# Local attention and a phase-mixing layer on one core: the last head pair of the first batch in two-head pieces, the first steps reordered, the weight loads reordered

## The chip, the core and the metric

The kernel runs on one core of a Trainium2 chip. The metric is the device time of one execution in microseconds. Four runs of the kernel before gave a median of 172.93 us, between 172.67 and 173.31 us. One further execution was recorded by the hardware profiler; it took 172.37 us, of which the span from the first to the last instruction is 170.2 us, so 2.2 us lie around the span.

The core has five engines that run side by side, each in the order of its own queue: the tensor engine (PE, with weight loads shown as PEld), the vector engine (DVE), the scalar engine (ACT), GpSimd (POOL) and SyncE (SP). They meet through semaphores. Transfers are issued by SP, ACT or POOL and run on sixteen shared DMA engines.

## What is computed

Four batches of 768 tokens. First an attention with 8 heads of 64 features, in which a token sees the 96 tokens before it and the first 8 tokens, with a bias that falls with distance. Then a layer that turns the result by angles, mixes it over tokens with two 768 x 768 matrices and over channels with a 512 x 512 matrix:

```python
scores = scale * q @ k.T + bias          # masked: local window of 96, or one of the first 8 keys
a = softmax(scores)
x = (a @ v)                              # B, S, H*D = 4, 768, 512
theta = x @ w_theta
zr, zi = x * cos(theta), x * sin(theta)
y = w_tok_r @ zr + w_tok_i @ zi          # over tokens
u = x + y
out = u + relu(u @ w_ch)
```

## The kernel before

Tokens are tiled in six tiles of 128 (`NT = 6`), heads in four pairs (`NP = 4`), the 512 channels in four blocks of 128 (`NC = 4`); pair `p` of heads fills channel block `p` of x.

The first batch is written out by hand, instruction by instruction, in the order of lines 535 to 618, and every engine keeps that order. Everything after it (the mixing of batch b woven with the attention of batch b+1) is ordered by a scheduler, apart from the last tiles.

For a pair `p` of the first batch the steps are these. `turn0` (L209) transposes q and k of two heads on PE, 12 transposes each, and `out0` (L213) copies the results out of PSUM as qT (on DVE) and kT (on ACT). `kglob` (L221) makes kG, copies of the key tiles whose first 8 columns are those of the global keys, with two DVE copies. Scores come in three chunks `c` of two token tiles: `score_bias` (L278) writes the bias into a PSUM tile with two matmuls, `score_mms` (L287) adds the products, `score_exp` (L309) takes the exponential on ACT. The chunks 0 and 1 take 8 score matmuls, the chunk 2 takes 6. `vglob` (L335) makes vG, the value tiles with the global rows, for four heads at a time with two DVE copies. `values` (L346) multiplies by the values for one head; a 65th column of ones gives the sum of the softmax, and DVE takes the reciprocal (`rec`, L371) and multiplies (`x_sb`, L373). `xtrans` (L375) transposes x of a pair on PE and copies it out of PSUM as xT. In batches 1 to 3 `xtrans` is a DMA transpose from the SP queue instead, except for the last pair of batch 1, which goes over PE and an ACT copy.

`theta` (L390) multiplies xT by w_theta, for two token tiles at a time: `theta(b, c, 2)` takes the channel blocks 0 to 2 and `theta(b, c, 3)` the last one, because the last pair of heads is the last to be ready. `sines` (L410) takes cosine and sine on ACT (`cs`) and multiplies by x on DVE (`zri`). `trans_w` (L165) transposes one row block of the two token matrices from `w_nat` on PE and copies it out as `w_tokT`. `mix` (L424) is the multiplication over tokens, `utrans` (L439) and `chan` (L451) the last step. The sine functions and the exponential need different tables on ACT; `sine_table` (L306) loads the one for sines with a dummy activation.

The weights are loaded by `load_w` (L153), from the POOL queue: w_theta first, then pairs of row blocks of the two token matrices, the q and k of batch 1, and w_ch. A load waits at its issue until the load eight places before it has landed. PSUM has four small tiles (`ps`, one bank each) and two large ones (`pb`, two banks each), handed out in turn; a step that takes one waits until its last reader is through.

Of the kernel before, what the change touches and what calls it, by code (L numbers as in the profile page):

```python
# [9 lines left out]
FP = mybir.dt.float32  # L10
# [6 lines left out]
def kernel(  # L17
# [13 lines left out]
    nc = tc.nc  # L31
    B, H, S, D = q.shape
    T = 128
    NT = S // T
    DM = H * D
    NC = DM // T
    NP = H // 2
# [18 lines left out]
    def ps_small(shape, dtype):  # L56
        return small.tile(shape, dtype, name="ps", tag="ps")
# [40 lines left out]
    for i_, eng in ((1, nc.sync), (0, nc.scalar)):  # L98
        eng.dma_start(out=qk32[:, i_].rearrange("p h t d -> p h (t d)"),
                      in_=(q, k)[i_][0, 0:2].rearrange("h (p t) d -> p h (t d)", p=T))  # L100
# [47 lines left out]
    w_theta_bf = const.tile([T, NC, DM], BF)  # L148
# [2 lines left out]
    w_tokT = [const.tile([T, NT, S], BF, name=f"w_tokT_{wi}") for wi in range(2)]  # L151

    def load_w():  # L153
        nc.gpsimd.dma_start(out=w_theta_bf, in_=moe_w_theta.rearrange("(c p) n -> p c n", p=T))
        for tt in range(0, NT, 2):
            for wi, src in enumerate((moe_w_tok_r, moe_w_tok_i)):
                w2 = moe.tile([T, 2, S], BF, name="w_nat", bufs=6)
                nc.gpsimd.dma_start(
                    out=w2, in_=src[tt * T:(tt + 2) * T, :].rearrange("(a p) s -> p a s", p=T))
                w_nat[wi, tt], w_nat[wi, tt + 1] = w2[:, 0], w2[:, 1]  # L160
            if tt == NT - 4:
                load_all_qk(1)
        nc.gpsimd.dma_start(out=w_ch_bf, in_=moe_w_ch.rearrange("(c p) n -> p c n", p=T))
# [29 lines left out]
    def behind(eng):  # L193

        return tc.issue_after(anchor[eng]) if eng in anchor else nullcontext()
# [17 lines left out]
    def out0(p, i_, copy, half=None):  # L213
        to = qkT.setdefault((0, p), [None, None, None])
        if to[i_] is None:
            to[i_] = att.tile([T, S], BF, name=("qT", "kT")[i_], tag=("qT", "kT")[i_], bufs=6)
        ns = slice(0, T) if half is None else slice(half * T // 2, (half + 1) * T // 2)
        copy(out=to[i_].rearrange("p (n t) -> p n t", t=NT)[:, ns],  # L218
             in_=tiles0[p, i_].rearrange("p t n -> p n t")[:, ns])

    def kglob(b, p, t0=0, t1=NT - 2, copy=nc.vector.tensor_copy):  # L221
        kT = qkT[(b, p)][1]
        if t0 == 0:
            qkT[(b, p)][2] = att.tile([T, NT - 2, T], BF, name="kG", bufs=6)
        kG = qkT[(b, p)][2][:, t0:t1]
        with behind("zri" if p else "dve") if b == B - 1 else nullcontext():
            copy(  # L227
                out=kG, in_=kT[:, (t0 + 1) * T:(t1 + 1) * T].rearrange("p (t n) -> p t n", t=t1 - t0))
            copy(out=kG[:, :, 0:NG], in_=kT[:, None, 0:NG].to_broadcast([T, t1 - t0, NG]))  # L229
# [48 lines left out]
    def score_bias(p, c):  # L278
        pb = pbs[0, p, c] = ps_big()
        n = min(4, 2 * NT - 1 - 4 * c)  # L280
        s0 = 2 if c else 0
        for hh in range(2):
            nc.tensor.matmul(pb[:, hh, 0:n * T], lhsT=diag[:, 2 * p + hh],
                             rhs=dist[:, s0:s0 + n].rearrange("p s n -> p (s n)"),
                             start=True, stop=False)
# [20 lines left out]
    def sine_table():  # L306
        nc.scalar.activation(junk, halfpi, AF.Sin)
# [25 lines left out]
    vGs, pos = {}, {}  # L333

    def vglob(b, h0, n):  # L335

        vn = loads[b][1]
        if h0 == 0:
            vGs[b] = att.tile([T, H, NT - 2, D + 1], BF, name="vG", bufs=1)
        hs = slice(h0, h0 + n)  # L340
        vG = vGs[b]
        with behind("dve"):
            nc.vector.tensor_copy(out=vG[:, hs], in_=vn[:, hs, 1:NT - 1, :])
        nc.vector.tensor_copy(out=vG[0:NG, hs], in_=vn[0:NG, hs, 0:1, :].to_broadcast([NG, n, NT - 2, D + 1]))

    def values(b, p, hh, i0=0, i1=NT):  # L346
        vn = loads[b][1]
        e_t, vG = ebuf[(b, p)], vGs[b]
        h = 2 * p + hh
        if b == 0:  # L350
            po = ps_small([T, 1, 512], FP)
        else:
            if hh == 0:
                pos[(b, p)] = ps_big()
            po = pos[(b, p)][:, hh:hh + 1, :]
        for it in range(i0, i1):
            mms = [(e_t[:, hh, it, 0, :], vn[:, h, it, :])]
            if it:
                mms.append((e_t[:, hh, it - 1, 1, :], vG[:, h, it - 2, :] if it > 1 else vn[:, h, 0, :]))
            o = po[:, 0, (it - i0) * (D + 1):(it - i0 + 1) * (D + 1)]  # L360
            for i_, (l_, r_) in enumerate(mms):
                nc.tensor.matmul(o, lhsT=l_, rhs=r_, start=(i_ == 0), stop=(i_ == len(mms) - 1))  # L362
        if b and hh == 0:
            return
        if b:
            po = pos[(b, p)]
        h0, n = (hh, 1) if b == 0 else (0, 2)
        nt = i1 - i0
        po4 = po[:, :, 0:nt * (D + 1)].rearrange("p a (t d) -> p a t d", d=D + 1)
        rec = att.tile([T, n, NT, 1], FP, name="rec", tag=f"rec{n}")[:, :, 0:nt]  # L370
        nc.vector.reciprocal(rec, po4[:, :, :, D:D + 1])  # L371
        xv = x_sb[b][:, p, i0:i1, h0 * D:(h0 + n) * D].rearrange("p t (a d) -> p a t d", a=n)
        nc.vector.tensor_mul(xv, po4[:, :, :, 0:D], rec.to_broadcast([T, n, nt, D]))  # L373

    def xtrans(b, p, copy=nc.vector.tensor_copy, i0=0, i1=NT):  # L375
        if b > 1 or (b and p < 3):
            anchor["sp"] = nc.sync.dma_start_transpose(
                out=xT_sb[b][:, p, :].rearrange("p (t s) -> p t s", t=NT),
                in_=x_sb[b][:, p].rearrange("p t d -> p (t d)")).ins
            return  # L380
        ps = ps_small([T, S], BF)
        own = slice(i0 * T, i1 * T)
        for st in range(i0, i1):
            nc.tensor.transpose(ps[:, st * T:(st + 1) * T], x_sb[b][:, p, st, :], ident)
        copy(out=xT_sb[b][:, p, own], in_=ps[:, own])
# [4 lines left out]
    def theta(b, c, j):  # L390
        last0 = [(j_, NC - 1) for j_ in range(2)]
        part = {0: [(0, dc) for dc in range(NC - 1)],
                1: [(1, dc) for dc in range(NC - 1)] + last0,
                2: [(j_, dc) for j_ in range(2) for dc in range(NC - 1)],
                3: last0}[j]
        if c == 0 and j in (0, 2):
            zri[b] = moe.tile([T, 2, NT, DM], BF, name="zri", tag="zri", bufs=1)
        xT, xb = xT_sb[b], x_sb[b]
        last = c == NT // 2 - 1
        if j in (0, 2):  # L400
            pss["th", c] = [ps_small([T, DM], FP) for _ in range(2)] if last else ps_big()
        pb = pss["th", c]
        st = lambda j_: slice((2 * c + j_) * T, (2 * c + j_ + 1) * T)
        for j_, dc in part:
            nc.tensor.matmul(pb[j_] if last else pb[:, j_, :], lhsT=xT[:, dc, st(j_)],  # L405
                             rhs=w_theta_bf[:, dc, :], start=(dc == 0), stop=(dc == NC - 1))
        if j == 1:
            sines(b, c)
# [59 lines left out]
    def load_all_qk(b):  # L468
        alloc_qk(b)
        load_qk(b, 0, 8)  # L470
# [63 lines left out]
    dve, act = nc.vector.tensor_copy, nc.scalar.copy  # L534
# [26 lines left out]
    for p in range(NP - 1):  # L561
        score_exp(0, p, 1)
        out0(p + 1, 1, act)
        out0(p + 1, 0, dve)
        kglob(0, p + 1)
        score_bias(p, 2)
        score_mms(0, p, 2)
        if p:
            values(0, p - 1, 0)
            values(0, p - 1, 1)  # L570
        score_exp(0, p, 2)
        if p < 2:
            vglob(0, 4 * p, 4)
        score_bias(p + 1, 0)
        score_mms(0, p + 1, 0)
        if p + 2 < NP:
            turn0(p + 2, 1)
            turn0(p + 2, 0)
        score_exp(0, p + 1, 0)
        score_bias(p + 1, 1)  # L580
        score_mms(0, p + 1, 1)
        if p == 1:
            xtrans(0, 0)
    p = NP - 1
    score_exp(0, p, 1)
    values(0, p - 1, 0)
    xtrans(0, p - 2)
    values(0, p - 1, 1)
    score_bias(p, 2)
    score_mms(0, p, 2)  # L590
    score_exp(0, p, 2)
    trans_w(0, act, False, act)
    sine_table()
    xtrans(0, p - 1, dve)
    values(0, p, 0, 0, 4)
    values(0, p, 1, 0, 4)
    theta(0, 0, 2)
    xtrans(0, p, dve, 0, 4)
    values(0, p, 0, 4, 6)
    values(0, p, 1, 4, 6)  # L600
    theta(0, 0, 3)
    xtrans(0, p, dve, 4, 6)
    sines(0, 0)
    theta(0, 1, 2)
    theta(0, 1, 3)
    theta(0, 2, 2)
    theta(0, 2, 3)
    trans_w(1, dve, True)
# [97 lines left out]
```

## Time and profile before

| what | value |
|---|---|
| four runs, median (lowest to highest) | 172.93 us (172.67 to 173.31) |
| profiled execution: time, span | 172.37 us, 170.2 us |
| PE busy, share of the span | 157.6 us, 93% |
| DVE busy | 125.9 us, 74% |
| ACT busy | 100.8 us, 59% |
| POOL busy | 37.8 us, 22% |
| DMA of the POOL queue (q0) | 12.45 MB in 45680 packets |
| DMA of the SP queue (q1) | 12.52 MB in 28176 packets |
| granted PE clock | full speed in all slices |

Times in the profile count from the start of the span. The page gives averages; which engine sets the end changes from stage to stage, so a change at one place is read from the waits of that stage: what starts when, and what it waited for. PE's matmuls overlap: one of 128x512 is shown with some 380 ns, but the next may start 216 ns after it, so gaps on PE are read from the starts.

### The profile page before, as it was taken

How to read it: one execution, taken by the hardware profiler on the slowest of the kernel's cores; microseconds unless marked ns; L12 is line 12 of the kernel's file. 1: busy time of each engine (PE TensorE's matmuls, PEld its weight loads, DVE VectorE, ACT ScalarE, POOL GpSimd, SP SyncE). 2: the span in 40 equal slices, each digit the busy share in tenths (PEclk: the TensorE clock that was granted, in tenths of full speed). 3: DMA queues.
4: the chain of work that ended last, by engine and by line, in shares of the span. 5: the costliest groups of instructions: out<-in, count | busy, mean ns of one | idle time of the engine just before them, and what ended most of it. 6: DMA issues, size and time to landing. Idle time of an engine off the chain costs nothing.

```text
span 170.2 us, 3718 instructions
## 1 busy us (share of the span) xinstructions
PE 157.6 (93%) x1516; PEld 84.2 (49%) x1540; DVE 125.9 (74%) x267; ACT 100.8 (59%) x129; POOL 37.8 (22%) x45
## 2 busy tenths in 40 slices
PE   7478998999999999999999999999999999999991
PEld 2255574565646456445555463444554644444440
DVE  6646976598999999967998788588776856614432
ACT  4697787997587576399944550899348309400010
POOL 8966347003192110497000000000000000000000
PEclk9999999999999999999999999999999999999999
DMA  4999999999999999999997678779145472222435
GB/s 152 201 173 178 208 209 203 206 208 179 151 205 183 190 141 179 127 156 196 145 119 86 140 171 129 166 139 262 35 77 139 112 168 78 111 60 43 148 92 185
DMA packets 74288, 25.73 MB, mean 151 GB/s; under 512 B 62368, under 2 KB 71328, under 8 KB 74272
## 3 DMA queue, kind: packets, MB, share of 16 engines
q0 software_dynamic: 45680, 12.45, 78.9%
q1 hardware_dynamic: 28176, 12.52, 33.2%
q10 hardware_dynamic: 416, 0.52, 1.0%
q8 instruction: 12, 0.20, 0.5%
q14 instruction: 4, 0.03, 0.1%
HBM read 25.69 MB, written 6.29 MB: 188 GB/s over the span
## 4 chain that ended last, share of the span: by engine, by line
PE 65%; DVE 19%; DMA 7%; ACT 6%; issue 1%; DVEq 0%
PE ps L430 30%; PE ps L458 9%; PE pb L405 7%; PE pb L303 5%; DMA xT<-x_sb 4%; PE ps L405 4%; PE pb L362 3%; DVE qT L257 3%; DMA qk<-in_k_dram 2%; DVE e L322 2%; ACT e L313 2%; DVE x_sb L373 2%; PE ps L207 2%; DVE e L325 1%; DVE kG L227 1%
## 5 line engine op out<-in xcount | busy, mean ns | idle before, releaser
L430 PE MATMUL ps<-zri,w_tokT 128*128 128x512 bf16 x273 | 67.7, 380 | 1.1 <-issue 0.3
L313 ACT ACTIVATE e<-pb 128x1024 bf16<-128x1024 f32 (+1 forms) x48 | 43.7, 954 | 18.4 <-PE pb L303 17.9
L430 PEld LDWEIGHTS <-w_tokT 128*128 128x128 bf16 x288 | 25.9, 98 | 28.1 <-DVE w_tokT L175 0.6
L435 DVE TENSOR_TENSOR u<-x_sb,ps 128x512 bf16<-128x512 bf16 x24 | 16.3, 680 | 11.0 <-PE ps L430 10.8
L458 PE MATMUL ps<-w_ch_bf,uT 128*128 128x512 bf16 (+1 forms) x97 | 24.2, 371 | 0.2
L419 DVE TENSOR_TENSOR zri<-x_sb,cs 128x1024 bf16<-128x1024 bf16 (+1 forms) x30 | 16.6, 581 | 6.5 <-ACT cs L415 6.4
L463 DVE SCALAR_TENSOR_TENSOR o_sb<-ps,u 128x512 f32<-128x512 f32 (+1 forms) x25 | 16.4, 663 | 4.1 <-PE ps L458 3.6
L415 ACT ACTIVATE cs<-pb,halfpi 128x1024 bf16<-128x1024 f32 x8 | 8.9, 1114 | 16.4 <-PE pb L405 16.4
L303 PE MATMUL pb<-qT,kT 64*128 64x128 bf16 x224 | 15.4, 220 | 2.4 <-DVE qT L218 1.3
L322 DVE TENSOR_TENSOR e<-e,etab 128x1024 bf16<-128x1024 bf16 (+1 forms) x24 | 14.8, 618 | 3.1 <-ACT e L313 3.0
L303 PEld LDWEIGHTS <-kT 64*128 64x128 bf16 x224 | 8.9, 94 | 14.9 <-issue 12.1
L405 PE MATMUL pb<-w_theta_bf,xT 128*128 128x512 bf16 x61 | 15.0, 380 | 1.0 <-DMA xT<-x_sb 0.6
L362 PEld LDWEIGHTS <-e 128*128 128x128 bf16 x352 | 12.8, 97 | 4.3 <-issue 1.8
L449 ACT COPY uT<-ps 128x512 bf16<-128x512 bf16 x7 | 4.2, 594 | 18.2 <-PE ps L448 18.2
L405 PEld LDWEIGHTS <-xT 128*128 128x128 bf16 x96 | 8.9, 98 | 12.1 <-DMA xT<-x_sb 2.1
L458 PEld LDWEIGHTS <-uT 128*128 128x128 bf16 x100 | 9.0, 98 | 9.7 <-ACT uT L449 0.8
L88 POOL DMA_DIRECT2D vn<-in_v_dram x5 | 9.6, 1928 | 14.1 <-DVE qkn L238 12.4
L303 PE MATMUL pb<-qT,kG 64*128 64x128 bf16 x128 | 11.5, 217 | 0.5 <-DVE kG L229 0.5
L373 DVE TENSOR_TENSOR x_sb<-pb,rec 128x768 bf16<-128x768 f32 x12 | 11.4, 953 | 0.3
L362 PE MATMUL pb<-vn,e 128*128 128x65 bf16 x168 | 9.7, 193 | 0.6 <-DVE x_sb L373 0.3
L325 DVE TENSOR_TENSOR e<-e,etab 128x1024 bf16<-128x1024 bf16 x12 | 8.2, 687 | 2.4 <-ACT e L313 2.4
L259 ACT COPY kT<-ps 128x768 bf16<-128x768 bf16 x8 | 6.4, 797 | 4.6 <-PE ps L253 4.4
(76 smaller groups left out, 203.1 us busy)
## 6 DMA issues: line engine op xcount, KB each, us to landing
out_dram<-o_sb SPq DMA_DIRECT2D x23, 256.0 KB, 2.4
vn<-in_v_dram POOLq DMA_DIRECT2D x3, 768.0 KB, 21.0
qk<-in_q_dram POOLq DMA_DIRECT2D x2, 768.0 KB, 20.6
qk<-in_k_dram POOLq DMA_DIRECT2D x2, 768.0 KB, 23.6
w_nat<-in_moe_w_tok_r_dram POOLq DMA_DIRECT2D x3, 384.0 KB, 14.8
w_nat<-in_moe_w_tok_i_dram POOLq DMA_DIRECT2D x3, 384.0 KB, 14.0
vn<-in_v_dram POOLq DMA_DIRECT2D x2, 384.0 KB, 9.7
qk<-in_q_dram POOLq DMA_DIRECT2D x8, 96.0 KB, 9.1
```

The source lines that it names most:

```text
L303: nc.tensor.matmul(pb[:, hh, o:o + T], lhsT=lhsT, rhs=qT[R, (own, nxt)[part]], start=bool(b), stop=bool(b) or (jt == NT - 1 or (j == 1 and ...
L313: ins = nc.scalar.activation(e_c, pb[:, :, 0:n], AF.Exp, scale=scale).ins
L322: nc.vector.tensor_mul(e_c, e_c, tab[:, :, s0:s0 + n // T].rearrange("p a s n -> p a (s n)"))
L325: nc.vector.tensor_mul(e4, e4, tab[:, :, 2:4].rearrange("p a s n -> p a (s n)")[:, :, None, :].to_broadcast([T, 2, 2, 2 * T]))
L362: nc.tensor.matmul(o, lhsT=l_, rhs=r_, start=(i_ == 0), stop=(i_ == len(mms) - 1))
L373: nc.vector.tensor_mul(xv, po4[:, :, :, 0:D], rec.to_broadcast([T, n, nt, D]))
L405: nc.tensor.matmul(pb[j_] if last else pb[:, j_, :], lhsT=xT[:, dc, st(j_)], rhs=w_theta_bf[:, dc, :], start=(dc == 0), stop=(dc == NC - 1))
L419: anchor["zri"] = nc.vector.tensor_mul(zri[b][:, i_, 2 * c + j_:2 * c + j_ + n, :].rearrange("p j (g d) -> p j g d", g=NP), xb[:, :, 2 * c ...
L430: anchor["pe"] = nc.tensor.matmul(ps, lhsT=w_tokT[wi][:, st, tt * T:(tt + 1) * T], rhs=zri[b][:, wi, st, :], start=(st == 0 and wi == 0), ...
L435: anchor["dve"] = nc.vector.tensor_add(u_sb[b, tt].rearrange("p (g d) -> p g d", g=NP), x_sb[b][:, :, tt, :], ps.rearrange("p (g d) -> p g ...
L458: nc.tensor.matmul(ps_c, lhsT=uT[:, dc, :], rhs=w_ch_bf[:, dc, i_ * n:(i_ + 1) * n], start=(dc == 0), stop=(dc == NC - 1))
L463: nc.vector.scalar_tensor_tensor(o_sb[:, cols], in0=ps_c, scalar=0.0, in1=u[:, cols], op0=ALU.max, op1=ALU.add)
```

## The change

The pieces of the diff:

- `load_w` issues the first row blocks of the two token matrices ahead of w_theta.
- `values` can take both heads of a pair at once (`hh` is None) for a range of tiles in one PSUM tile, with one reciprocal and one multiplication. The last pair of batch 0 uses it in three pieces of two token tiles, instead of one piece of four tiles and one of two for each head.
- `theta` has two new parts, 4 (channel blocks 0 and 1) and 5 (block 2). For the first two token tiles they run apart, around the first two pieces of the last pair. Part 2 goes over the blocks with the two token tiles inside, not the other way round.
- In the loop over pairs, `turn0` of the next but one pair stands after the scores of chunk 1 of the next pair; for pair 3 the qT copy stands before the xT copy of pair 0, and the second `vglob` after kG of pair 3 (it stood before both).
- After the loop, the transposes of pair 1 stand behind the scores of the last chunk, and their copy is on ACT instead of DVE; the sine table is loaded ahead of the copies of `trans_w(0)`.
- `xtrans` takes the last pair of batch 2 over PE and an ACT copy as well; it was a DMA transpose.

```diff
     def load_w():
-        nc.gpsimd.dma_start(out=w_theta_bf, in_=moe_w_theta.rearrange("(c p) n -> p c n", p=T))
         for tt in range(0, NT, 2):
...
                 w_nat[wi, tt], w_nat[wi, tt + 1] = w2[:, 0], w2[:, 1]
+            if tt == 0:
+                nc.gpsimd.dma_start(out=w_theta_bf, in_=moe_w_theta.rearrange("(c p) n -> p c n", p=T))
...
     def values(b, p, hh, i0=0, i1=NT):
...
-        h = 2 * p + hh
+        nt = i1 - i0
         if b == 0:
-            po = ps_small([T, 1, 512], FP)
+            h0, n = (0, 2) if hh is None else (hh, 1)
+            po4 = ps_small([T, 512], FP)[:, 0:n * nt * (D + 1)].rearrange("p (a t d) -> p a t d", a=n, d=D + 1)
...
+        for head in range(2) if hh is None else (hh,):
+            h = 2 * p + head
+            for it in range(i0, i1):
...
     def xtrans(b, p, copy=nc.vector.tensor_copy, i0=0, i1=NT):
-        if b > 1 or (b and p < 3):
+        if b > 2 or (b and p < NP - 1):
...
-                2: [(j_, dc) for j_ in range(2) for dc in range(NC - 1)],
-                3: last0}[j]
+                2: [(j_, dc) for dc in range(NC - 1) for j_ in range(2)],
+                3: last0,
+                4: [(j_, dc) for dc in range(NC - 2) for j_ in range(2)],
+                5: [(j_, NC - 2) for j_ in range(2)]}[j]
...
     for p in range(NP - 1):
         score_exp(0, p, 1)
         out0(p + 1, 1, act)
-        out0(p + 1, 0, dve)
+        if p < 2:
+            out0(p + 1, 0, dve)
         kglob(0, p + 1)
+        if p == 2:
+            vglob(0, 4, 4)
         score_bias(p, 2)
         score_mms(0, p, 2)
         if p:
             values(0, p - 1, 0)
             values(0, p - 1, 1)
         score_exp(0, p, 2)
-        if p < 2:
-            vglob(0, 4 * p, 4)
+        if p == 0:
+            vglob(0, 0, 4)
         score_bias(p + 1, 0)
         score_mms(0, p + 1, 0)
+        score_exp(0, p + 1, 0)
+        score_bias(p + 1, 1)
+        score_mms(0, p + 1, 1)
         if p + 2 < NP:
             turn0(p + 2, 1)
             turn0(p + 2, 0)
-        score_exp(0, p + 1, 0)
-        score_bias(p + 1, 1)
-        score_mms(0, p + 1, 1)
         if p == 1:
+            out0(3, 0, dve)
             xtrans(0, 0)
     p = NP - 1
     score_exp(0, p, 1)
     values(0, p - 1, 0)
-    xtrans(0, p - 2)
-    values(0, p - 1, 1)
     score_bias(p, 2)
     score_mms(0, p, 2)
     score_exp(0, p, 2)
+    xtrans(0, p - 2, act)
+    values(0, p - 1, 1)
+    sine_table()
     trans_w(0, act, False, act)
-    sine_table()
-    xtrans(0, p - 1, dve)
-    values(0, p, 0, 0, 4)
-    values(0, p, 1, 0, 4)
-    theta(0, 0, 2)
-    xtrans(0, p, dve, 0, 4)
-    values(0, p, 0, 4, 6)
-    values(0, p, 1, 4, 6)
+    xtrans(0, p - 1)
+    values(0, p, None, 0, 2)
+    theta(0, 0, 4)
+    xtrans(0, p, dve, 0, 2)
+    values(0, p, None, 2, 4)
+    theta(0, 0, 5)
     theta(0, 0, 3)
-    xtrans(0, p, dve, 4, 6)
-    sines(0, 0)
+    xtrans(0, p, dve, 2, 4)
+    values(0, p, None, 4, 6)
     theta(0, 1, 2)
     theta(0, 1, 3)
+    sines(0, 0)
+    xtrans(0, p, dve, 4, 6)
     theta(0, 2, 2)
     theta(0, 2, 3)
     trans_w(1, dve, True)
```

More of the change, by code (lines that the diff above doesn't have):

```diff
@@ L348, in values @@
         e_t, vG = ebuf[(b, p)], vGs[b]
-        h = 2 * p + hh
+        nt = i1 - i0
         if b == 0:
-            po = ps_small([T, 1, 512], FP)
+            h0, n = (0, 2) if hh is None else (hh, 1)
+            po4 = ps_small([T, 512], FP)[:, 0:n * nt * (D + 1)].rearrange("p (a t d) -> p a t d", a=n, d=D + 1)
         else:
+            h0, n = 0, 2
             if hh == 0:
                 pos[(b, p)] = ps_big()
[L355 to L362, printed above, removed]
+            po4 = pos[(b, p)][:, :, 0:nt * (D + 1)].rearrange("p a (t d) -> p a t d", d=D + 1)
+        for head in range(2) if hh is None else (hh,):
+            h = 2 * p + head
+            for it in range(i0, i1):
+                mms = [(e_t[:, head, it, 0, :], vn[:, h, it, :])]
+                if it:
+                    mms.append((e_t[:, head, it - 1, 1, :], vG[:, h, it - 2, :] if it > 1 else vn[:, h, 0, :]))
+                for i_, (l_, r_) in enumerate(mms):
+                    nc.tensor.matmul(po4[:, head - h0, it - i0], lhsT=l_, rhs=r_,
+                                     start=(i_ == 0), stop=(i_ == len(mms) - 1))
         if b and hh == 0:
             return
[L365 to L369, printed above, removed]
         rec = att.tile([T, n, NT, 1], FP, name="rec", tag=f"rec{n}")[:, :, 0:nt]
@@ L393, in theta @@
                 1: [(1, dc) for dc in range(NC - 1)] + last0,
-                2: [(j_, dc) for j_ in range(2) for dc in range(NC - 1)],
-                3: last0}[j]
-        if c == 0 and j in (0, 2):
+                2: [(j_, dc) for dc in range(NC - 1) for j_ in range(2)],
+                3: last0,
+                4: [(j_, dc) for dc in range(NC - 2) for j_ in range(2)],
+                5: [(j_, NC - 2) for j_ in range(2)]}[j]
+        if c == 0 and j in (0, 2, 4):
             zri[b] = moe.tile([T, 2, NT, DM], BF, name="zri", tag="zri", bufs=1)
@@ L399, in theta @@
         last = c == NT // 2 - 1
-        if j in (0, 2):
+        if j in (0, 2, 4):
             pss["th", c] = [ps_small([T, DM], FP) for _ in range(2)] if last else ps_big()
```

## The prediction

> **What bounds the kernel now.** I read the chain that ended last, in order of time, then the timeline of each stretch that the change touches. The chain's lines have start, duration, engine and tile:
>
> ```profile
> 15.70 0.46 DVE kG L227
> 16.18 0.18 DVE kG L229
> 16.41 0.23 PE pb L303 x2
> ...
> 41.55 0.96 DVE qT L257
> ...
> 66.00 0.86 DVE x_sb L373
> ...
> 66.89 3.79 DMA xT<-x_sb
> 70.72 0.39 PE pb L405
> ...
> 103.18 3.33 DMA xT<-x_sb
> 106.56 2.33 PE pb L405 x10
> ```
>
> The hand-written stage runs to about 41 us, mostly PE with hand-overs to DVE and ACT. From 41.55 to 66.86 the chain is DVE without a break. Then a DMA transpose brings x of batch 1, pair 2, then PE, then a DMA transpose for batch 2, pair 3. All three places matter: a gain in the first stage must pass the second and the transfer behind it. The timeline of PE shows the end of the first stage; brackets give idle time and releaser:
>
> ```profile
> 24.24 0.51 PE L384 MATMUL ps<-ident,x_sb 128*128 128x128 bf16 x6
> ...
> 25.08 0.28 PE L362 MATMUL ps<-vn,e 128*128 128x65 bf16 x4
> ...
> 27.50 0.61 PE L405 MATMUL pb<-w_theta_bf,xT 128*128 128x512 bf16 x2 [0.28 <-DVE xT L385]
> 28.30 0.29 PE L384 MATMUL ps<-ident,x_sb 128*128 128x128 bf16 x2 [0.20 <-DVE x_sb L373]
> 28.42 1.89 PE L405 MATMUL pb<-w_theta_bf,xT 128*128 128x512 bf16 x8
> 30.15 1.89 PE L405 MATMUL ps<-w_theta_bf,xT 128*128 128x512 bf16 x8
> 31.88 0.83 PE L171 MATMUL pbw<-ident,w_nat 128*128 128x128 bf16 x12
> ```
>
> Starts give what PE needs: a theta matmul 0.216 us (eight from 28.42 to 30.15), six transposes 0.34 (68.94 to 69.28), eight value matmuls 0.25 (26.81 to 27.06), a `turn0` pair 0.79 (12.18 to 12.97), a bias 0.54, eight scores 0.33. A hand-over takes 0.04 us from PE and 0.06 to PE.
>
> **Stage to 24 us: earlier scores.** Before, ACT idles from 13.31 to 13.95 because chunk 1 of pair 1 stands behind `turn0` on PE. Ahead of it, bias and scores run from 12.18 to 13.05, so the exponential starts at 13.2, the kT copy of pair 2 ends at about 15.0 (before 15.66) and kG at 15.7 (before 16.35). PE's work is only reordered: it reaches the kG matmuls at 15.93 as it did and no longer waits until 16.41. Gain 0.48. From there PE has no gap, so the same swap for pair 3 moves the exponentials but nothing on PE.
>
> DVE at 17.7: qT(3) and xT(0) come first, kG(3) ends at 19.7, before PE asks at 20.0; the two vG copies (0.43 + 0.42) end at 20.5, before `values` of pair 2 at 21.2. Nothing, covered by 0.7 (0.85 at most without it). But the vG copies now stand ahead of x of pair 1, which ends at 22.0, as before (21.99). PE does the last scores first (to 22.29), transposes pair 1 (to 22.63), then values and `trans_w(0)` to 23.64. DVE needs 0.19 + 0.56 for x of pair 2 after 22.97, and the transposes of pair 2 start at 24.04, not 24.24. Of the 0.48 us, 0.20 are left. They also wait for their PSUM tile, now freed by ACT's xT copy: 0.80 us (the row at 69.49) from 23.13, so 23.93: hidden by 0.1, and 1:1 beyond. Behind it stand all of PE's work and hence theta.
>
> **Stage 24 to 32 us: three pieces.** Before: 7.64 us from 24.24 to 31.88, with three waits: 24.83 to 25.08 (a small PSUM tile held by ACT's w_tokT copy), 27.06 to 27.50, 27.92 to 28.30, together 1.07; work 6.57. The matmuls stay the same in number. After, the first piece waits for xT(2) to be copied (to 25.15), a reciprocal 0.17 and a multiplication 0.42 (the row of 128x256), to 25.75, while PE has theta blocks 0 and 1 until 25.43: 0.32. The second piece's copy hides behind block 2; its wait is 0.04. So 24.04 + 6.57 + 0.36 = 30.97 instead of 31.88: gain 0.91. DVE has 3 x (0.17 + 0.42 + 0.29) = 2.64 us for the last pair, before 2.79.
>
> Covers here: the sine table (1.28 + 0.20) ahead of the w_tokT copies (1.50 for both) leaves ACT free at 26.8; their tiles are wanted at 27.03 (the first copy ends at 26.1) and 29.13, and the cosine at 27.2 (before 28.14). The third piece's xT copy now stands behind four `zri` multiplications, which ended 2.82 us after the cosine's start, so at 30.0; the copy ends at 30.3, PE wants it at 30.55: 0.2 of cover.
>
> **Loads.** w_theta is issued third. Landings before: w_theta 8.54 + 11.4 = 19.9, then the two token blocks 21.8 and 23.7; the queue lands them in order at a steady rate, so w_theta now lands third, at 23.7 (bounds: its old 19.9, and 27.5, where the load two places behind landed). It is wanted at 24.57: cover 0.85. In POOL's queue it passes only those two loads. The batch 1 v load, which waited for the third load, still does.
>
> **From 41 us: does it pass?** The DVE stretch moves as a whole, if its loads are there: v of batch 1 lands at 24.56 + 23.2 = 47.8, its copy ran at 48.89 and would at 47.98. More than 1.05 us can't pass. Then the SP queue:
>
> ```profile
> 57.28 1.94 SPq L377 DMA_TRANSPOSE xT<-x_sb  x1
> 59.27 0.57 SPq L465 DMA_DIRECT2D out_dram<-o_sb  x1
> 60.23 7.87 SPq L377 DMA_TRANSPOSE xT<-x_sb  x2
> ```
>
> The transposes at 57.28 and 60.23 landed after 8.1 and 8.0 us, the third (66.89) after 3.8, one issued at 94.2 after 2.7. POOL's loads, some 200 GB/s from 17 us on, hold the DMA engines until 69.1 and don't move with the compute. In the packets the first transpose begins at 61.9, the second ends at 67.6, the third runs from 68.0 (1.1 after its issue) to 70.3. If the first two stay put, the third starts at 67.6: 0.4 passes. If its 3.8 us move with the issue, 0.9 passes; if it stays behind the loads, nothing; a loss would need more loads in front of it, and none is added. I take 0.6, between the first two.
>
> "DMA: Bandwidth & Descriptors" in the Trainium skill, section "Queues, rings and completion order", says that an engine takes turns between the queues it has work for, packet by packet. The 4.6 us between issue and first packet do not look like that; by the rule alone the 0.9 would pass, 171.8 us in all.
>
> **Batch 2, pair 3 over PE and ACT.**
>
> ```profile
> 104.67 1.49 PE L405 MATMUL pb<-w_theta_bf,xT 128*128 128x512 bf16 x5
> 106.56 2.33 PE L405 MATMUL pb<-w_theta_bf,xT 128*128 128x512 bf16 x10 [0.41 <-DMA xT<-x_sb]
> ```
>
> Six theta matmuls from 104.67 end at 105.97 and the next waits until 106.56: 0.59. After, PE adds six transposes, 0.34. They stand behind three of the eight mixing matmuls at 102.08, so at 102.73; x is ready at 101.68 + 0.96 = 102.64, cover 0.03; if x is later, the five mixing matmuls, the channel step and theta behind them on PE wait 1:1. ACT's copy (0.80) lies in a hole of 6.9 us and ends at 104.1, long before it is wanted. Gain 0.59 - 0.34 = 0.25 (bounds: 0.59, were the transposes hidden, and -0.34, were the DMA). SP loses one transpose of 1.79 us; the uT and the batch 3 kT and qT behind it come earlier, which nobody waits for: the next step in the chain is ACT's.
>
> "VectorE: DVE Perf Modes", section "The three transpose paths", speaks against this: 390 ns for a 128x128 transpose on TensorE. Six would be 2.34 us (an estimate from that page) and the swap a loss of 1.75. The rows at 68.94 have six starts in 0.34 us; they decide.
>
> **Sum.** -0.6 - 0.25 = -0.85 us, from 172.37 to 171.52 in the profiled execution's terms. The median lies 0.56 above it: 172.08, say 172.1 us.
>
> **Rivals.**
> - A, the transfer moves with its issue: -0.91 - 0.25, so 171.8. For it: at 66.89 the queue in front was nearly empty (1.1 us to the first packet). Against: the first two transposes waited out the loads.
> - B, the transfer stays at 70.68 and swallows the first stage: -0.25, so 172.7. For it: two landings 8 us after their issue. Against: 0.4 us between 67.6 and 68.0 without a packet of that queue.
> - C, slower: w_theta lands late. Place: the first theta matmul at 24.57; price 1:1 beyond 24.6, less 0.3 of waits that then vanish; with batch 2 it turns to a loss from 26.0. At the bound of 27.5, 24.04's stretch ends at 33.6 instead of 31.88: +1.7 - 0.25, so 174.4. For it: POOL's landings spread from 11.4 to 19.1 us. Against: their steady 1.9 us steps.
> - D, the covers of 0.1 to 0.25 us (ACT's copy, the third piece's xT) are used up together: first stage 0.4, all of it passing, so 172.3; it lies inside the range.
>
> **How the numbers follow.** Forecast with D 0.48, A 0.25, B 0.17, C 0.10. What this kernel's measurement can tell from no change is 0.3%, 0.52 us, so faster means below 172.41. The forecast is below it in 17 of 20 cases, A always, B hardly, C never: faster 0.66, same 0.23, slower 0.11. The forecast's own range is 171.7 to 172.5; with A (up to 0.6 below its time) and B (up to 0.3 above), 171.2 to 173.0 leaves out C and the edges.
>
> **What would show it.** Transposes of pair 2 near 24.0; the last theta matmul of the first stage near 30.8 and `trans_w(1)` near 31.0; the first cosine near 27.2; no wait on the DMA at the first theta matmul; the DVE stretch from about 40.6; the third transpose's landing between 69.8 and 70.3; no DMA wait near 106. It is wrong if PE waits for w_theta, if the first stage gains under 0.5, or if the DVE stretch grows for its loads.

## The result, and the profile after

| | before | after |
|---|---|---|
| median (lowest to highest, runs) | 172.86 us (171.85 to 173.78, 63) | 172.31 us (171.70 to 173.37, 44) |
| ratio, 95% interval | | 0.997 (0.9962 to 0.9979) |
| profiled execution: time, span | 172.37 us, 170.2 us | 172.37 us, 170.3 us |

The change is worth 0.55 us; 0.85 was forecast. The two profiled executions took the same time, so the profile after has to be read stage by stage, and with one offset: its first scores start at 8.46 us instead of 8.15, so the times of PE's work below carry 0.31 us that are not the change's (a second profile of the kernel before, e8, starts at 8.51).

The timeline of PE after, the end of the first stage (start, duration, engine, line, operation, idle time before it and who ended it):

```profile
16.24 0.22 PE L304 MATMUL pb<-qT,kG 64*128 64x128 bf16 x2
...
24.29 0.51 PE L384 MATMUL ps<-ident,x_sb 128*128 128x128 bf16 x6 [0.21 <-DVE x_sb L373]
...
26.00 0.28 PE L384 MATMUL ps<-ident,x_sb 128*128 128x128 bf16 x2 [0.16 <-DVE x_sb L373]
...
29.47 1.89 PE L407 MATMUL ps<-w_theta_bf,xT 128*128 128x512 bf16 x8
31.20 0.83 PE L172 MATMUL pbw<-ident,w_nat 128*128 128x128 bf16 x12
```

`trans_w(1)` starts at 31.20 instead of 31.88. The stretch from the transposes of pair 2 to it took 6.91 us instead of 7.64, with two short waits left. The chain that ended last shows what became of it:

```profile
25.68 23.18 DMA vn<-in_v_dram
48.88 0.70 DVE vG L344
...
66.47 4.56 DMA xT<-x_sb
...
71.08 0.39 PE pb L407
...
105.54 3.45 PE pb L407 x16
```

Two entries are new or longer. The v load of batch 1 now stands on the chain (DVE waits 0.59 us for it at 48.88). And the transposing transfer of batch 1's pair 2, issued at 66.47 instead of 66.89, takes 4.56 us instead of 3.79: PE goes on at 71.08, later than the 70.72 of before. The first stage's gain is there at 31 us and gone at 71. The timeline of PE shows it as a wait, first after, then before:

```profile
69.09 1.03 PE L460 MATMUL ps<-w_ch_bf,uT 128*128 128x512 bf16 x4
71.08 1.25 PE L407 MATMUL pb<-w_theta_bf,xT 128*128 128x512 bf16 x4 [0.96 <-DMA xT<-x_sb]
```

```profile
69.51 1.03 PE L458 MATMUL ps<-w_ch_bf,uT 128*128 128x512 bf16 x4
70.72 2.12 PE L405 MATMUL pb<-w_theta_bf,xT 128*128 128x512 bf16 x8 [0.19 <-DMA xT<-x_sb]
```

Before, PE's own work ended only 0.19 us ahead of that transfer. After, it ends 0.96 us ahead. Batch 2's part did as forecast: theta runs through from 105.37 (the chain enters it at 105.54) to 108.99, where before it stopped for 0.41 us. From batch 1's theta matmuls to the first `chan` matmul behind batch 2's it takes 37.75 us (71.08 to 108.83), before 38.00 (70.72 to 108.72). The SP queue of after, to compare with the three lines of before:

```profile
56.87 1.65 SPq L377 DMA_TRANSPOSE xT<-x_sb  x1
58.58 0.57 SPq L467 DMA_DIRECT2D out_dram<-o_sb  x1
59.81 7.88 SPq L377 DMA_TRANSPOSE xT<-x_sb  x2
```

All three transposes are issued 0.41 to 0.42 us earlier, and the third lands 0.36 us later.

### The profile page after: what moved, and what is told of

Its sections match the earlier page's. It is cut to its first block, busy times and chain, and to the rows that moved or that the text cites. A ratio compares the mean times of both kernels' runs of the same rounds, so it can differ in the third digit from the quotient of the medians.

```text
span 170.3 us, 3728 instructions
## 1 busy us (share of the span) xinstructions
PE 158.3 (93%) x1521; PEld 84.8 (50%) x1546; DVE 124.9 (73%) x265; ACT 102.2 (60%) x131; POOL 37.6 (22%) x45
## 4 chain that ended last, share of the span: by engine, by line
PE 59%; DMA 19%; DVE 13%; ACT 6%; issue 1%; DVEq 0%
PE ps L432 26%; DMA vn<-in_v_dram 14%; PE ps L460 9%; PE pb L407 6%; PE pb L304 5%; PE pb L366 3%; PE ps L407 3%; DMA xT<-x_sb 3%; DMA qk<-in_k_dram 3%; DVE e L323 2%; ACT e L314 2%; DVE x_sb L373 2%; DVE e L326 1%; PE ps L208 1%; ACT cs L417 1%
```

## The experiments

Medians of 12 runs each unless said otherwise; the ratio is to the kernel before on the same chip at the same time, with its 95% interval. In the text the kernels go by the short names e1 to e12.

### e1, e2: one part at a time

e1 is the kernel before with the batch 2 part alone, e2 the changed kernel without it.

```diff
e1, in the kernel before:
-        if b > 1 or (b and p < 3):
+        if b > 2 or (b and p < NP - 1):
e2, in the changed kernel:
-        if b > 2 or (b and p < NP - 1):
+        if b > 1 or (b and p < NP - 1):
```

> The kernel before with one part of the change alone: pair 3 of batch 2 is transposed on TensorE and copied by ScalarE instead of by the transposing transfer. Theory A (my working: this part gives 0.25 us by itself, the first stage passes the rest): 0.15 to 0.35 us less than before, about 172.6; the chain reaches batch 2's theta matmuls without a wait for xT, and the L458 matmuls behind them start about 0.25 earlier. Theory B (the whole gain of 0.55 is the first stage's, this part only trades a wait for work): within 0.1 us of before. Theory C (the first stage's gain is swallowed whole, this part carries all): 0.45 to 0.65 us less.

> The changed kernel without its batch 2 part: pair 3 of batch 2 goes through the transposing transfer as before. Theory A: 0.2 to 0.4 us less than before, about 172.55. Theory B: 0.45 to 0.65 less, about 172.3. Theory C: within 0.1 us of before, 172.86. By all three the second token block starts its transposes at 30.9 to 31.2 us instead of 31.88, and what differs is how much of that is left at the theta matmuls of batch 1 (70.7 in the profile before).

Measured: e1 172.43 us, ratio 0.9988 (0.9974 to 1.0002), about -0.24 in the middle: theory A's number, though the interval reaches no change. e2 173.35 us, ratio 1.0038 (1.0020 to 1.0057): slower than before by 0.68, which none of the three theories had. The parts don't add: -0.24 and +0.68, together -0.55. With the batch 2 part in, the first stage brings 0.31 (0.9988 to 0.9970; the two intervals overlap, and together they leave anything from 0 to 0.6). Without the first stage the batch 2 part brings 0.24, with it 1.2 (1.0038 to 0.9970). Where e2 loses shows in its timeline of PE at batch 2:

```profile
104.57 1.46 PE L407 MATMUL pb<-w_theta_bf,xT 128*128 128x512 bf16 x5
107.20 1.04 PE L407 MATMUL pb<-w_theta_bf,xT 128*128 128x512 bf16 x4 [1.18 <-DMA xT<-x_sb]
```

It comes to theta 0.10 us earlier than before (104.57 against 104.67) and then waits 1.18 us for the transfer instead of 0.41. That transfer was issued at 103.09 and took 4.07 us; before, 103.18 and 3.33.

### e3, e6: the loads

e3 restores the old load order. e6 moves the last pair of token weight loads behind batch 1's v.

```diff
e3:
     def load_w():
+        nc.gpsimd.dma_start(out=w_theta_bf, ...)
...
-            if tt == 0:
-                nc.gpsimd.dma_start(out=w_theta_bf, ...)
e6 (`load_w` takes a range; `w_ch` ends its first call):
...
-    load_w()
+    load_w(0, NT - 2)
     load_all_v(1)
+    load_w(NT - 2, NT)
```

> The changed kernel with the load of the theta weights first again. Theory D (the order makes batch 1's v late: its issue waits for the third load, which is now the larger one): v of batch 1 lands near 47.8 instead of 48.9, its vG copy doesn't wait (0.59 us in the profile after), and the time falls by 0.1 to 0.4 us to about 172.0, unless the second token block, third again and wanted at 23.6, comes later than that and gives it back. Theory E (the first of the 16 engines to finish a load did so at the same time in both profiles, 22.1 us for the third load, and only the last one was 1.1 us later in the profile after, so it is that execution and not the order): v lands anywhere between 47.8 and 48.9 in either order, and the time is within 0.15 us of the changed kernel's 172.31, or later by up to 0.5 us by the second token block.

> The changed kernel with the last two token weight loads behind batch 1's v instead of ahead of the channel weights: v is issued near 22.5 us instead of 25.7 and should land near 45.5 instead of 48.9, so its copy can't wait. Theory L (the landing of batch 1's transfer is set by later loads and swallows what comes before it): within 0.15 us of the changed kernel's 172.31, though x_sb of pair 2 is ready 0.3 to 0.6 us earlier. Theory V (the 0.59 us wait for v is what took the first stage's gain): 0.3 to 0.6 less, about 171.85.

Measured: e3 172.28 us, ratio 0.9978 (0.9964 to 0.9991), the changed kernel's time. In its profile v landed at 48.26 and its copy did not wait (PE waited 0.23 us for the second token block at 24.21, in place of the 0.21 that it waits for x of pair 2 in the profile after); in e1, with the old order, v landed at 48.59; in e2, with the new one, at 47.86. So theory E: the order is worth nothing that these runs resolve, and the landing of v moves by a microsecond from one execution to the next. e3 also shows that v is not what binds: x of pair 2 was ready at 66.02, earlier than in any profile so far, and PE then stood all the longer:

```profile
70.98 1.69 PE L406 MATMUL pb<-w_theta_bf,xT 128*128 128x512 bf16 x6 [1.29 <-DMA xT<-x_sb]
```

e6 was a miss: 176.87 us, ratio 1.0255 (1.0229 to 1.0280, 6 runs). It was built on the token weights of row block 4 being wanted at 51 us; they are transposed at 41.0 in the profile after, and now PE waited for them:

```profile
45.42 0.82 PE L173 MATMUL ps<-ident,w_nat 128*128 128x128 bf16 x6 [4.29 <-DMA w_nat<-in_moe_w_tok_r_dram]
```

It says nothing on theories L and V; it shows that the tail of this load queue has no room for a swap.

### e4, e10, e9: without the transfer of batch 1's pair 2

e4 takes pair 2 of batch 1 over PE and ACT too. e10 is e4 again, run beside e9, which is the kernel before with both transfers gone, that is e4 less the first stage.

```diff
e4 and e10, in the changed kernel:
-        if b > 2 or (b and p < NP - 1):
+        if b > 2 or (b and p < NP - 1 and (b, p) != (1, 2)):
e9, in the kernel before:
-        if b > 1 or (b and p < 3):
+        if b > 2 or (b and p < NP - 1 and (b, p) != (1, 2)):
```

> The changed kernel with pair 2 of batch 1 transposed on TensorE and copied by ScalarE too. Theory F (the transfer of this pair, 4.56 us from issue to landing, is what takes the first stage's gain: TensorE stands 0.96 us before the theta matmuls at 71.08): that wait goes, TensorE pays 0.34 us for six transposes and ScalarE one copy of 0.6 to 0.8; 0.3 to 0.8 us less than the changed kernel, about 171.8. Theory G (VectorE's chain of batch 1 or ScalarE's queue is as late as the transfer): within 0.15 us of 172.31, with the wait now put down to VectorE's x_sb or ScalarE's copy. Worse by 0.2 to 0.5 if ScalarE's copy pushes the exponentials of pair 3.

> e4 once more, the changed kernel with batch 1's pair 2 on TensorE too, on the same chip as e9. By both theories 171.7 to 172.1, 0.3 to 0.6 us under the changed kernel.

> The kernel before with batch 1's pair 2 and batch 2's pair 3 both transposed on TensorE and copied by ScalarE: e4 less the first stage. Theory L (the first stage's gain was there all along and only the transfer of batch 1's pair 2, which ends with the load queue, swallowed it): without that transfer the first stage is worth 0.7 to 1.0 us, so this takes 172.6 to 172.9 against 171.9 of e4. Theory W (something else of batch 1, VectorE's chain or the wait for v, takes it as well): this is within 0.4 us of e4, 172.0 to 172.3.

Measured: e4 171.89 us, ratio 0.9949 (0.9929 to 0.9969); e10 171.89 us, 0.9951 (0.9930 to 0.9971); e9 173.21 us, 1.0026 (1.0000 to 1.0052). e4 beats both kernels, the one before by 0.8 to 0.9 us and the changed one by about 0.35 (0.9970 against 0.9949 and 0.9951), as theory F had it. Between e9 and e10 the first stage (with the load order) is the only difference, and it is worth 1.3 us in the medians, 0.7 to 1.9 by the intervals. Theory L's 0.7 to 1.0 lies at the lower end of that; theory W's 0.4 at most lies outside. Both profiles start alike (first scores at 8.16 and 8.14). The timeline of PE, e9 first, at the end of the first stage and at batch 1's theta:

```profile
32.63 0.56 PE L171 MATMUL pbw<-ident,w_nat 128*128 128x128 bf16 x7
...
71.00 1.24 PE L405 MATMUL pb<-w_theta_bf,xT 128*128 128x512 bf16 x5
```

```profile
31.72 0.83 PE L172 MATMUL pbw<-ident,w_nat 128*128 128x128 bf16 x12
...
69.76 2.54 PE L407 MATMUL pb<-w_theta_bf,xT 128*128 128x512 bf16 x11
```

0.91 us at `trans_w(1)`, 1.24 at theta, and no wait in front of it in either. So the first stage's gain goes through all of batch 1's attention (by the chains DVE until 57 us, then mostly PE), and only the transfer takes it. The 0.33 that are added on the way are one copy of vG, 1.01 us in e9 and 0.69 in e10 (more on it at the end). e9 also shows that e4's edit alone brings the kernel before nothing: there PE comes to theta by its own work as late as with the transfer (71.00 against 70.72 and 71.22 in before and e1), and the edit only adds work.

### e5, e11: what sets the transfer's landing

Reading the landings out of the traces gives this, for the transfer of batch 1's pair 2, for the last of those POOL loads that are issued before the gate of `load_behind` (which holds the second half of batch 3's loads back until an xT of batch 1 is there), and for the 16 KB of code that the instruction queue fetches near that time:

| kernel | transfer issued | last early load landed | code fetch ended | transfer landed | after the load | PE waited |
|---|---|---|---|---|---|---|
| before | 66.89 | 69.96 | 69.09 | 70.68 | 0.72 | 0.19 |
| e8 (before again) | 67.02 | 70.41 | 69.46 | 71.19 | 0.78 | 0.58 |
| e1 | 67.52 | 70.45 | 69.56 | 71.17 | 0.72 | 0 |
| after | 66.47 | 70.39 | 69.03 | 71.04 | 0.65 | 0.96 |
| e2 | 66.36 | 69.97 | 68.98 | 70.57 | 0.60 | 0.62 |
| e3 | 66.05 | 70.13 | 68.24 | 70.93 | 0.80 | 1.29 |
| e7 | 67.42 | 70.29 | 69.40 | 71.01 | 0.72 | 0 |
| e12 | 68.69 | 72.08 | 71.00 | 72.60 | 0.52 | 0 |
| e5 | 65.87 | 62.13 | 64.92 | 68.63 | - | 0 |
| e11 | 65.87 | 62.75 | 65.31 | 68.63 | - | 0 |
| e6 | 71.76 | 68.10 | 71.09 | 74.50 | - | 0 |

In the first seven rows the issue moves by 1.5 us, the landing by 0.6, and it keeps to the loads. e12, a run that started late and in which the transfer before this one landed only at 71.88, comes closer to them. The loads' end is not this transfer's doing: in e9, e10 and e4, which do without it, the last early load landed at 69.94, 70.42 and 70.31.

The code fetch is a rival that stays. In before, e1, e2, e7 and e12 the transfer lands 1.59 to 1.61 us after the end of the fetch, which is closer than it keeps to the loads. In the profile after and in e3 it lands 2.01 and 2.69 us after the fetch, but 0.65 and 0.80 after the loads: there the fetch alone can't be what holds it.

e5 moves those loads away; e11 is e5 with two more u on PE.

```diff
e5:
-            side.append((0, lambda: (alloc_qk(3), load_qk_tokens(3, 0, H // 2))))
+            side.append((0, lambda: alloc_qk(3)))
...
-            load_qk_tokens(b, H // 2, H // 2)
+            load_qk_tokens(b, 0, H)
e11, on top of it:
-        if (b or b) and (b, tt) != (B - 1, NT - 1):
+        if b and (b, tt) not in ((1, 0), (1, 1), (B - 1, NT - 1)):
```

> The changed kernel with the first half of batch 3's token loads (eight of 192 KB, issued from 46 to 63 us) moved behind the gate with the other half. In five profiles the transfer of batch 1's pair 2 landed 0.60 to 0.80 us after the last packets of the loads issued before the gate (69.97 to 70.57, 69.96 to 70.68, 70.13 to 70.93, 70.39 to 71.04, 70.45 to 71.17), however early its input was ready (66.0 to 67.5). Theory L (those loads set that landing): the transfer lands 2.5 to 3.5 us after its issue, near 69.3, the wait of 0.96 us before the theta matmuls of batch 1 shrinks to under 0.3, and the time falls by 0.5 to 0.9 us to about 171.6. Theory K (the code fetch of 16 KB, which runs from 68.0 to 69.0 in all of them, holds the transfer): it lands 1.6 us after the end of that fetch, 70.6, and the time falls by at most 0.35. Worse by 0.5 or more if the loads behind the gate, twice as many now, come too late for batch 3's transposing transfers at 97.

> e5 (batch 3's early token loads behind the gate) with batch 1's first two u transposed on TensorE and copied by ScalarE, as batch 0's are, since in the profile of e5 the transfer of one of them took 8.90 us (86.95 to 95.85, the end of batch 3's v load) and TensorE's chain went over it. Theory L: nothing on TensorE's path goes through a transfer while loads run; e5's gain of 1.4 us at batch 1's theta matmuls (start offset taken out) less 0.44 for eight transposes and up to 0.3 at batch 2 is left: 171.2 to 171.8. Rival (TensorE is full from 70 us on, and what is moved to it is paid in full): 171.9 to 172.3, no better than e4 or e5.

Measured: e5 172.16 us, ratio 0.9959 (0.9933 to 0.9985). Its profile is as theory L had it at the place: the transfer landed at 68.63, 2.76 us after its issue, and theta started without a wait:

```profile
69.35 3.18 PE L407 MATMUL pb<-w_theta_bf,xT 128*128 128x512 bf16 x14
```

It doesn't part theory L from theory K, because the fetch had moved too, to 64.0; what speaks against the fetch alone are the rows of after and e3. e11 and e6 agree with both (2.76 and 2.74 us, loads and fetch over before the issue). But the time is hardly below the changed kernel's. The chain and PE's timeline say where it went:

```profile
86.95 8.90 DMA uT<-u
```

```profile
95.89 1.04 PE L460 MATMUL ps<-w_ch_bf,uT 128*128 128x512 bf16 x4 [0.79 <-DMA uT<-u]
```

The loads are now in front of another transfer: that of u landed at 95.85, when batch 3's v load ended at 96.02. The collision was moved, not removed. e11 takes that transfer away as well, and was a miss: 173.66 us, ratio 1.0057 (1.0034 to 1.0081). Both theories had it faster. PE waited in new places (1.2 us for ACT's exponentials after 80 us, whose chain now holds a uT copy, and 0.5 us for u): from 80 to 100 us PE was busy for 18.38 of 20 us, 19.99 in e10.

### e7, e8, e12: why the first stage alone is slower

In the trace of e2 a code fetch of 16 KB runs from 104.3 to 105.5, in the middle of the late transfer; in that of before from 103.0 to 103.9, one transfer earlier on the same queue. e7 and e12 lengthen PE's instruction stream, to move the fetch; e8 is the kernel before once more, for a second profile.

```diff
e7, in e2; e12, in the kernel before:
-            nc.tensor.matmul(ps, lhsT=zero[:, 0:T], rhs=zero, start=True, stop=True)
+            nc.tensor.matmul(ps[:, 0:T], lhsT=zero[:, 0:T], rhs=zero[:, 0:T], start=True, stop=True)
...
-    warm(6)
+    warm(18)
```

> The first stage alone (e2) with the 6 warm-up matmuls of 512 columns at the start replaced by 18 of 128 columns: the same time on TensorE ahead of its first work, and 24 more instructions in its stream, so that every code fetch of 16 KB that TensorE's stream takes comes 24 instructions earlier, 1 to 2.6 us. Theory K2 (first stage alone is slower because the code fetch, at 104.3 to 105.5 us in its profile, falls on the transfer of batch 2's pair 3, which lands at 107.16 instead of 106.51): the fetch comes at 101.7 to 103.3, the transfer lands at 105.5 to 106.5, and the time falls by 0.5 to 1.2 us to 172.2 to 172.9. Rival (that transfer is late for another reason, the order on its queue or the first stage itself): the time stays at 173.35 within 0.3.

> The kernel before once more, for a second profile of it. Theory K2: if the code fetch near 103 us comes again at 103.0 the transfer of batch 2's pair 3 lands again near 106.5; if it comes at 104.3 as in the other profiles, the transfer lands near 107.1 and the run is up to 0.6 us longer. Rival (where the fetch falls doesn't matter): 106.5 wherever it falls. The transfer of batch 1's pair 2 lands 0.6 to 0.8 us after the last early load, as in all the others.

> The kernel before with the same 18 short warm-up matmuls as e7 in place of 6 long ones: the stream of TensorE is 24 instructions longer ahead of everything. In both profiles of the kernel before the code fetch near 103 us started 32.3 us after the waiting theta matmul of batch 1 (103.0 after 70.72, 103.5 after 71.24), held pair 2's transfer of batch 2 (landed by 105.07 and 105.59 instead of 103.2) and, one behind the other on the queue, pair 3's. Theory K2: the fetch starts 30.7 to 31.3 us after that matmul, pair 3's transfer lands 0.4 to 1.3 us earlier relative to it (35.8 in both profiles before), TensorE's wait of 0.41 there goes, and the time falls by 0.2 to 0.45 us, less up to 0.5 if TensorE warms up later by the shorter matmuls (its first scores start at 8.66 in the profile of e7). Rival (where the fetch falls doesn't matter): the landing stays at 35.8 after that matmul.

Measured: e7 172.56 us, ratio 1.0000 (0.9983 to 1.0017), 0.4% under e2, as theory K2 had it. e8, one run of 172.76 us, and e12 173.18 us, 1.0017 (0.9993 to 1.0041), where K2 had expected a gain of up to 0.45 less a late start. The profiles, with times against the first theta matmul of batch 2 (that of e12 is of a run with a late start, so only differences are used):

| kernel | code fetch starts | transfer lands | PE's wait |
|---|---|---|---|
| before | -1.65 | +1.84 | 0.41 |
| e8 | -1.67 | +1.85 | 0.41 |
| e12 | -1.73 | +1.84 | 0.41 |
| e7 | -1.73 | +1.83 | 0.42 |
| e2 | -0.25 | +2.59 | 1.18 |

Where the fetch comes one transfer earlier the wait is 0.41 or 0.42, in four profiles; in the one where it comes in the transfer itself it is 1.18. That the two go together is shown by one profile of e2 only. What K2 got wrong is the handle: 24 more instructions did not move the fetch by 1 to 2.6 us in e12, it came at the same place against the work. And e7 changed more than the fetch: with the short warm-up its first stage ends a microsecond later (`trans_w(1)` at 32.51, in e2 at 31.52). So e7 undid e2's loss, but whether by the fetch or by the later first stage isn't separated, and why e2's fetch came 1.4 us later than the others stays open; the number of PE instructions ahead of that theta differs by one between before and e2 (2224 and 2223, with one matmul counted for each weight load).

## Why the prediction was right, point by point

**Stage to 24 us.** As forecast: transposes of pair 2 at 24.29, less the offset of 0.31 23.98, forecast 24.04. The kG matmuls start at 16.24, less the offset 15.93, without the wait that they had.

**24 to 32 us.** As forecast: 6.91 us where 6.93 was worked out, and 0.91 us at `trans_w(1)` between e9 and e10, the same as the sum (1.06 between e1 and e2).

**Loads.** Right that nothing waits for w_theta, wrong on the cover. It landed at 24.77 in the profile after and the first theta matmul started at 24.82: cover 0.05 us, not 0.85 (0.17 to 1.64 in seven other profiles with the new order). The step that failed is the steady rate, taken from one execution: the same third place landed at 23.66 in before and 24.51 in e1, both in the old order. The order may have a part in it: the third place averages 24.0 in six profiles with the old order and 24.5 in eight with the new one, and the two ranges overlap. Rival C was closer than its chance. For the same reason v of batch 1, put at 47.8, landed anywhere from 47.71 to 48.86, and in the profile after DVE waited 0.59 us for it, a wait that the prediction had ruled out below a gain of 1.05. e3 without that wait is no faster.

**Does it pass?** The term that was mis-sized. 0.6 of 0.91 was taken; 0.31 was measured on top of the batch 2 part, between rival B's nothing and the lower of the two bounds (0.4), though the intervals leave anything from about nothing to the forecast's 0.6. The prediction let the third transfer begin when the second ended. It did begin earlier, at 67.65 instead of 68.06 in the profile after, but the loads that it shares the engines with landed at 70.39 instead of 69.96 (the prediction had their end at 69.1), and it landed at 71.04. The table shows what it keeps to: 0.5 to 0.8 us after the last early load in eight profiles. What still passes, as far as these profiles tell, is what PE had been late by itself: the wait before was 0.19 us in one profile, 0.58 in another, 0 in e1, and where it was 0 the first stage pays until the transfer becomes the later one. Rival B had the mechanism; the "0.4 us without a packet" held against it was no room.

On the Trainium skill's page "DMA: Bandwidth & Descriptors", section "Queues, rings and completion order", the prediction noted that turns between queues, packet by packet, would let 0.9 pass. By e5 the transfer does land 2.76 us after its issue when the loads (and the code fetch) are gone, and 4.56 with them: sharing stretches it, and 0.31 passed.

**Batch 2, pair 3.** Right in size, -0.24 against -0.25, in the kernel before, and in the profile after the stretch from batch 1's theta to behind batch 2's is shorter by the same 0.25 us. The sum took the terms as independent, and they are not: on the first stage alone this edit is worth 1.2 us, since it removes the transfer at which e2 loses. The total came out within its range because the edit that was made removes that risk; the prediction did not know of it, and that is luck.

**Sum.** 172.08 forecast, 172.31 measured. The gain was 0.55 instead of 0.85, and the 0.30 between them are the part of the passing that did not come (0.6 - 0.31 = 0.29); the kernel before, at 172.86 in 63 runs instead of 172.93 in four, takes 0.07 off the difference in time.

## What to carry to other kernels

A gain passes a transfer only if the transfer's end moves with its issue: compare landings over several profiles with the last landing of the bulk loads on the other queue before counting on it, and if they keep together, take the operand of the critical step off that queue (e4) or the gain stays there. Where two paths end within 0.2 us of each other, shortening one of them alone is worth next to nothing; e9 and e10 show 1.3 us (0.7 to 1.9) for a stage that brought 0.3 (0 to 0.6) behind the transfer. Parts of a change that meet at one queue have to be run apart as well as together, since -0.24 and +0.68 made -0.55 here.

## What the runs showed of the hardware

The sixteen engines of a load do not finish together, and the spread varies from execution to execution: by the sixteen semaphore updates of the third weight load the first engine finished at 21.99 to 22.29 us in all profiles, the last at 23.66 (before) to 24.77 (after). A cover read off one profile's landing is good to a microsecond here.

The first copy of vG in batch 1 takes 0.69 to 0.71 us or 1.01 to 1.02. In before it is the long one, and POOL was issuing a load when it started:

```profile
48.54 0.84 POOL L82 DMA_DIRECT2D qk<-in_q_dram  x1
...
48.89 1.01 DVE L343 COPY vG<-vn 128x2080 bf16<-128x2080 bf16 x1
```

So it is in all eight profiles with the long time, with 0.34 to 0.36 us between the two starts. In the six with the short time POOL was idle when the copy started. But in e4, e9 and e10 a vG copy near 70 us started 0.16 or 0.17 us into such an issue, took 0.70, and the issue took 1.27 instead of 0.82. The Trainium skill's page "SBUF — State Buffer", section "SBUF: two separate sides", says that the port pair shared by DVE (in an operation that uses two ports) and GpSimd is locked for a whole instruction by the one that starts first, and that the other fully blocks. That one of the two loses time agrees, the rest doesn't: in before the copy was slowed by 0.31 us and not by the 0.5 us that were left of POOL's issue (to 49.38), and near 70 us the one that had started first lost. POOL's late issue in the profile after (1.29 us behind the one before it) is no sign of a lock: in after, e3, e4 and e10 that issue starts 0.31 us after the landing of v, whether the copy starts 0.02 or 0.20 us after it.

The granted clock dips in some executions and not in others, in the slice from 8.5 to 12.8 us of the span: 5 or 6 tenths in the profiles of e1, e2, e3, e9 and e10, full in before and after (in the traces half for 3.4 us, from 8.4 to 8.8 us on). e1 runs the same program as before up to batch 2 and has `trans_w(1)` at 32.58 instead of 31.88. Stage times of single profiles were therefore compared between pairs with the same dip (e9 and e10) or with the offset taken out.

The dip is also an experiment that nobody planned: 0.70 us are lost by the end of the first stage, and the question is again what of it reaches the end. Of the runs without a profile only the mean granted clock is on record, 0.99 or less in some and 0.995 or more in the others; that a run of the first group has its dip at this place is taken from the profiles (all at 0.99 or less have it, but for e6). In the changed kernel the medians of the two groups are 172.34 and 172.29 us (13 and 31 runs; means apart by 0.15 +- 0.22). In e4 and e10 together, where the transfer of batch 1's pair 2 is gone, they are 172.29 and 171.64 (11 and 13 runs; 0.67 +- 0.30). So a loss seems to be swallowed by the transfer as a gain is, and to go through where the transfer is gone. In the other experiments the groups are too small to tell.
